# Weight loads moved to ScalarE's DMA ring, two blocks loaded ahead of the weights, a new order

## The chip, the cores and the metric

The kernel runs on one core of a Trainium2 chip. The metric is the device time of a run in microseconds (us), the median of several runs. A profiled run also has a span, from its first to its last instruction, which is about 1.9 us shorter than the time.

## The reference

```python
# attention: a recurrent state per head, (4, 8, 768, 48) inputs
state = alpha[t] * state + outer(k[t], v[t]);  y[t] = q[t] @ state
# then, with x = y as (3072, 384):
h = x @ w_in                  # w_in (384, 2048)
g = s * relu(h)**2 + b
out = g @ w_out               # w_out (2048, 384)
```

## The kernel before

The sequence is cut into 24 blocks of 128 steps, and two blocks make a group. A block needs its four inputs a (alpha), q, k and v, each 192 KB. On ScalarE it goes through `ln` and `exp`, on VectorE through the products with q and k, on TensorE (PE) through several small matmuls, and ScalarE evicts (copies out of PSUM) its y to `xd`. A group of two such blocks then goes through `mm1` (h_ps from xd and w_in), `relu`, square and `mm2` (o_ps from w_out). The weights arrive as four w_in quarters i0 to i3 and four w_out quarters o0 to o3, 768 KB each, in four staging buffers `wst`, and ScalarE casts each to bf16. An o quarter can be loaded when the cast of the i quarter in its buffer is done.

All loads are issued by SyncE, so they stand in one ring, the queue of transfers that an engine's DMA issues go into:

```python
    def load(n, src, dst):                       # block n
        nc.sync.dma_start(out=dst[n % NIN], in_=src[...])          # cut
    for src, dst in ((alpha, a_in), (q, q_in), (k, k_in), (v, v_in)):
        load(0, src, dst)
    nc.scalar.dma_start(out=b_col, in_=moe_b.to_broadcast((128, 1)))
    nc.scalar.dma_start(out=s_col, in_=moe_s.to_broadcast((128, 1)))
    def load_w_in(i, st):
        nc.sync.dma_start(out=wst[st]..., in_=moe_w_in[...])        # cut
    def load_w_out(i, st):
        nc.sync.dma_start(out=wst[st]..., in_=moe_w_out[...])       # cut
LOADS = ["b0", "i0", "i1", "b1", "i2", "b2", "b3", "i3", "o0", "o1", "o2", "o3", "b4", ...]
```

A small list scheduler at build time (`op(engine, duration, priority, function, ...)`) decides the order of each engine's instructions. Every engine then works through its own list strictly in order. Where the scheduler sees PE idle early on, it lays "fills", matmuls of zeros into o_ps that are meant to keep PE's clock up.

(A transfer has landed when its last byte has arrived and its semaphore says so.)

## Time and profile before

| | before |
|---|---|
| time | 197.4 us (196.1 to 197.5, 3 runs) |
| span of the profiled run | 195.6 us |
| PE busy | 176.8 us, of which 58 fills are 10.7 us |
| first `ln`, first mm1, first mm2 | 4.19, 22.04, 34.3 us |

The page of the kernel before, cut to PE's total, PE's granted clock and the DMA engines' busy share (tenths, in 40 slices of the span), and the group of the fills (count, then busy us and mean ns):

```profile
PE 176.8 (90%) x2126; PEld 127.6 (65%) x2126; DVE 147.8 (76%) x353; ACT 108.7 (56%) x225; POOL 35.1 (18%) x60
...
PEclk9999999999999999999999999999999999999999
DMA  5999899987999998997699988999799799410012
...
L674 PE MATMUL o_ps<-zeros,ident_bf 128*128 128x256 bf16 x58 | 10.7, 338 | 0.0
```

PE looks busy nearly everywhere, but in the first slices that is fills. The windows view of the same run, by stage (busy us of each engine, then granted clock, DMA share and GB/s):

```profile
core 0: us, PE busy (x) PEld busy (x) DVE busy (x) ACT busy (x) POOL busy (x), PEclk, DMA share, GB/s
0.00:22.00 22.00, 14.06 (x148) 9.69 (x149) 9.90 (x20) 9.75 (x15) 7.87 (x23) 1.00 0.85 209
22.00:32.00 10.00, 8.18 (x118) 6.40 (x117) 9.14 (x23) 7.50 (x15) 2.06 (x3) 1.00 1.04 270
32.00:45.00 13.00, 10.97 (x106) 7.66 (x104) 11.26 (x26) 11.47 (x18) 2.22 (x2) 1.00 0.95 260
45.00:187.00 142.00, 138.43 (x1730) 101.02 (x1729) 115.28 (x282) 79.97 (x178) 22.99 (x33) 1.00 0.85 161
```

Taking the union of PE's matmul times without the fills (overlapping times counted once), PE loses 16.1 us before 22 us, 4.5 us from there to 45, and 3.6 us in the 142 us after. So the body is bound by PE, and the front by loads. The timeline of ScalarE (start, duration, and in brackets the idle time before it and what ended it):

```profile
0.77 0.57 ACTq L202 DMA_DIRECT2D b_col<-in_moe_b_dram  x1
1.37 0.61 ACTq L203 DMA_DIRECT2D s_col<-in_moe_s_dram  x1
4.19 0.52 ACT L298 ACTIVATE la<-a_in 128x384 bf16<-128x384 f32 x1 [2.17 <-DMA a_in<-in_alpha_dram]
...
14.14 0.51 ACT L298 ACTIVATE la<-a_in 128x384 bf16<-128x384 f32 x1
...
21.49 0.49 ACT L466 ACTIVATE xd<-py_ps 128x384 bf16<-128x384 f32 x1
```

The second block's y is evicted at 21.49 us, and mm1 follows (timeline of PE):

```profile
22.04 2.16 PE L488 MATMUL h_ps<-xd,w_in_bf 128*128 128x256 bf16 x16
```

### The profile page before, as it was taken

Reading aid. Unit: us, or ns where it says so; the run is one execution under the profiler, and the core shown is the slowest. Engines: PE = TensorE matmul, PEld = TensorE weight load, DVE = VectorE, ACT = ScalarE, POOL = GpSimd, SP = SyncE. Lnnn points to the kernel's source line nnn. Section 1 sums busy time; section 2 is a strip of 40 time slices with the busy share of each in tenths; the row PEclk is TensorE's granted clock in tenths of the full one; section 3 lists DMA queues with packets and bytes.
Section 4 is the critical chain, followed back from the end, with each engine's and each line's share of the span. In section 5 each row is a group of like instructions: output and inputs, shape, how many; then the busy total and the mean of one; then the engine's idle time right before and its main releaser. Section 6 shows DMA issues by size and latency. Waiting matters only on the chain.

```text
span 195.6 us, 5398 instructions
## 1 busy us (share of the span) xinstructions
PE 176.8 (90%) x2126; PEld 127.6 (65%) x2126; DVE 147.8 (76%) x353; ACT 108.7 (56%) x225; POOL 35.1 (18%) x60
## 2 busy tenths in 40 slices
PE   0698888699998899999999799998999999999992
PEld 0466666466666767777777577676676677776861
DVE  4434699699888999798987978737898889675541
ACT  3171877895135756567467477247367267365520
POOL 8401321005103033020121220301030232000000
PEclk9999999999999999999999999999999999999999
DMA  5999899987999998997699988999799799410012
GB/s 112 269 246 256 168 241 371 335 161 168 200 205 221 200 186 156 209 186 146 135 207 164 165 178 163 200 202 167 155 221 144 169 222 157 97 40 28 16 42 80
DMA packets 123161, 34.16 MB, mean 175 GB/s; under 512 B 116480, under 2 KB 121600, under 8 KB 123136
## 3 DMA queue, kind: packets, MB, share of 16 engines
q1 hardware_dynamic: 107008, 29.89, 68.4%
q10 hardware_dynamic: 16128, 3.94, 14.4%
q8 instruction: 16, 0.26, 0.5%
q14 instruction: 9, 0.07, 0.1%
HBM read 25.17 MB, written 4.72 MB: 153 GB/s over the span
## 4 chain that ended last, share of the span: by engine, by line
PE 66%; DMA 12%; DVE 8%; SPq 6%; ACT 5%; issue 2%; ACTq 0%; DVEq 0%
PE o_ps L512 28%; PE h_ps L488 25%; SPq L194 5%; DMA wst<-in_moe_w_out_dram 5%; PE py_ps L442 5%; DMA qkT<-qk 4%; DMA wst<-in_moe_w_in_dram 3%; PE a_ps L404 3%; DVE gt L505 3%; PE ct_ps L304 2%; ACT r L497 2%; ACT w_out_bf L263 1%; PE py_ps L362 1%; DVE t L387 1%; DVE qkT L371 1%
## 5 line engine op out<-in xcount | busy, mean ns | idle before, releaser
L497 ACT ACTIVATE r<-h_ps 128x512 bf16<-128x512 f32 x96 | 55.8, 599 | 35.0 <-PE h_ps L488 17.9
L512 PE MATMUL o_ps<-w_out_bf,gt 128*128 128x384 bf16 x384 | 71.9, 326 | 1.9 <-ACT w_out_bf L263 1.8
L488 PE MATMUL h_ps<-xd,w_in_bf 128*128 128x256 bf16 x576 | 72.5, 272 | 1.2 <-ACT r L497 0.9
L505 DVE TENSOR_TENSOR gt<-r 128x256 bf16<-128x256 bf16 x192 | 54.7, 333 | 16.1 <-ACT r L497 15.7
L488 PEld LDWEIGHTS <-w_in_bf 128*128 128x128 bf16 x576 | 54.5, 98 | 11.6 <-issue 1.9
L512 PEld LDWEIGHTS <-gt 128*128 128x128 bf16 x384 | 35.8, 98 | 21.7 <-issue 1.9
L413 DVE TENSOR_TENSOR am<-a_ps,mask 128x1024 bf16<-128x1024 f32 x24 | 29.3, 1220 | 1.5 <-PE a_ps L404 1.1
L398 POOL TENSOR_TENSOR s_st<-t,blast 128x384 bf16<-128x384 bf16 x16 | 14.6, 914 | 68.3 <-DVE t L387 51.1
L325 POOL CAST vp<-v_in 128x384 bf16<-128x384 f32 x24 | 15.2, 632 | 62.4 <-DMA v_in<-in_v_dram 57.0
L466 ACT ACTIVATE xd<-py_ps 128x384 bf16<-128x384 f32 x24 | 11.8, 491 | 22.0 <-PE py_ps L442 20.1
L336 DVE TENSOR_TENSOR qk<-k_in,binv 128x384 bf16<-128x384 f32 x24 | 14.2, 591 | 8.5 <-ACT binv L321 6.8
L523 DVE SCALAR_TENSOR_TENSOR o_sb<-o_ps,s_col,bias_w 128x384 f32<-128x384 f32 x24 | 14.8, 615 | 7.2 <-PE o_ps L512 6.5
L298 ACT ACTIVATE la<-a_in 128x384 bf16<-128x384 f32 x24 | 12.5, 522 | 5.5 <-DMA a_in<-in_alpha_dram 3.8
L321 ACT ACTIVATE binv<-ct_ps 128x384 f32<-128x384 f32 x24 | 11.8, 492 | 4.5 <-PE ct_ps L309 4.3
L331 DVE TENSOR_TENSOR qk<-q_in,b_s 128x384 bf16<-128x384 f32 x24 | 13.9, 580 | 0.4 <-ACT b_s L318 0.2
L318 ACT ACTIVATE b_s<-ct_ps 128x384 f32<-128x384 f32 x24 | 12.1, 503 | 2.0 <-issue 2.0
L387 DVE TENSOR_TENSOR t<-py_ps,s_st 64x192 bf16<-64x192 f32 x32 | 11.3, 354 | 2.5 <-PE py_ps L362 2.0
L404 PE MATMUL a_ps<-qkT 64*128 64x128 bf16 x192 | 9.7, 222 | 3.6 <-DVE qkT L371 2.4
L304 PE MATMUL ct_ps<-la,U_bf 128*128 128x384 bf16 x24 | 8.0, 335 | 4.9 <-ACT la L298 4.9
L404 PEld LDWEIGHTS <-qkT 64*128 64x128 bf16 x192 | 5.5, 95 | 10.0 <-DVE qkT L371 4.5
L442 PE MATMUL py_ps<-am,vp 128*32 128x128 bf16 x384 | 9.8, 223 | 1.5 <-DVE am L413 1.5
L674 PE MATMUL o_ps<-zeros,ident_bf 128*128 128x256 bf16 x58 | 10.7, 338 | 0.0
(42 smaller groups left out, 107.6 us busy)
## 6 DMA issues: line engine op xcount, KB each, us to landing
a_in<-in_alpha_dram SPq DMA_DIRECT2D x24, 192.0 KB, 3.7
q_in<-in_q_dram SPq DMA_DIRECT2D x24, 192.0 KB, 3.8
k_in<-in_k_dram SPq DMA_DIRECT2D x24, 192.0 KB, 4.0
v_in<-in_v_dram SPq DMA_DIRECT2D x24, 192.0 KB, 3.9
out_dram<-o_sb SPq DMA_DIRECT2D x24, 192.0 KB, 2.1
wst<-in_moe_w_in_dram SPq DMA_DIRECT2D x4, 768.0 KB, 6.5
wst<-in_moe_w_out_dram SPq DMA_DIRECT2D x4, 768.0 KB, 8.9
qkT<-qk ACTq DMA_TRANSPOSE x15, 4.5
```

The source lines that it names most:

```text
L325: nc.gpsimd.tensor_copy(out=vp_sb[n % 4].rearrange("a p (x d) -> a p x d", d=D)[:, :, 0:3:2, :], in_=v_in[n % NIN].rearrange("a (p e) d -> ...
L331: nc.vector.tensor_tensor(out=qk_sb[n % 3][:, 0, :, 0:D], in0=q_in[n % NIN], in1=b_sb[n % 2], op=ALU.mult)
L336: nc.vector.tensor_tensor(out=qk_sb[n % 3][:, 1, :, 0:D], in0=k_in[n % NIN], in1=binv_sb[n % 2], op=ALU.mult,)
L398: nc.gpsimd.tensor_tensor(out=s_sb[n % 3], in0=t1_sb[n % 2], in1=bl, op=ALU.mult)
L404: nc.tensor.matmul(out=a_ps[:, e, p, :], lhsT=qkT[64 * e : 64 * e + 64, 1, p, :], rhs=qkT[64 * e : 64 * e + 64, 0, p, :], start=True, stop ...
L413: nc.vector.tensor_tensor(out=am_sb[n % 2].rearrange("a e p t -> a (e p) t"), in0=a_ps.rearrange("a e p t -> a (e p) t"), in1=mask.unsquee ...
L442: nc.tensor.matmul(out=y_ps[32 * (x % 4) : 32 * (x % 4) + 32, x // 4, :], lhsT=(st[:, p, c0 : c0 + 32] if e is None else vp[:, p, c0 + 48 ...
L488: nc.tensor.matmul(out=hp[:, i * n : (i + 1) * n], lhsT=w_in_bf[:, kk, 128 * j : 128 * (j + 1)], rhs=xd_sb[g % 3][:, kk, 0:n], start=(kk = ...
L497: nc.scalar.activation(out=r_sb[w % 2], in_=h_ps[w % 2], func=AF.Relu)
L505: nc.vector.tensor_tensor(out=gt_sb[j][:, c0 : c0 + n], in0=r, in1=r, op=ALU.mult)
L512: nc.tensor.matmul(out=op[:, 0:d_model], lhsT=gt_sb[j][:, c0 : c0 + C], rhs=w_out_bf[:, j, :], start=(j == 0), stop=(j == NJ - 1),)
L523: nc.vector.scalar_tensor_tensor(out=ots, in0=o_ps[(x // 4) % 2][:, 0:d_model], scalar=s_col, in1=bias_w, op0=ALU.mult, op1=ALU.add,)
```

## The change

The intent: give the weights a ring of their own, so that they and the blocks no longer queue behind each other on SyncE's ring; load two blocks ahead of the first quarter, so that the attention part starts early; move the two scalars out of the way; and a re-tuned order.

```diff
-UNIT = 1.396
-LEAD = {1: 72.9, 2: 87.9, 4: 83.9}
-NPE = 9
-NAY = 5
+UNIT = 5.886
+LEAD = {1: 52.5, 2: 71.9, 4: 230.0}
+NPE = 7
+NAY = 10
-TB = 1.1
-TW = 2.3
+TB = 1.02
+TW = 2.15
 # ... (cut: every priority in P has another value)
-LOADS = ["b0", "i0", "i1", "b1", "i2", "b2", "b3", "i3", "o0", "o1", "o2", "o3", "b4", "b5", "b6"]
+LOADS = ["b0", "b1", "i0", "i1", "b2", "i2", "b3", "i3", "o0", "o1", "o2", "o3", "z0", "b4", "b5", "b6"]
-    nc.scalar.dma_start(out=b_col, in_=moe_b.to_broadcast((128, 1)))
-    nc.scalar.dma_start(out=s_col, in_=moe_s.to_broadcast((128, 1)))
     def load_w_in(i, st):
-        nc.sync.dma_start(
+        nc.scalar.dma_start(
     def load_w_out(i, st):
-        nc.sync.dma_start(
+        nc.scalar.dma_start(
+    def load_bs():
+        nc.sync.dma_start(out=b_col, in_=moe_b.to_broadcast((128, 1)))
+        nc.sync.dma_start(out=s_col, in_=moe_s.to_broadcast((128, 1)))
-            op("SP", TW, t, load_w_in, i, st, w=[("wst", st)], lat=2.0)
+            op("ACT", 0.5, t, load_w_in, i, st, w=[("wst", st)], lat=0.0)
+            op("SP", TW, t, lambda: None, r=[("wst", st)], w=[("wst", st)], lat=2.0)
 # ... (cut: the same for w_out, and the op for the scalars)
```

Two details of the scheduler's side: it models an issue on ScalarE as 0.5 us, and it models the transfer as if all loads still went one after another in the order of LOADS. `NPE` is the number of blocks whose transposes PE does; the others use DMA transposes.

More of the change, by code (lines that the diff above doesn't have):

```diff
@@ L18 @@
 GROUPS = [2, 2, 2, 2, 2, 2, 2, 2, 2, 2, 2, 2]
-UNIT = 1.396
-LEAD = {1: 72.9, 2: 87.9, 4: 83.9}
-NPE = 9
-NAY = 5
+UNIT = 5.886
+LEAD = {1: 52.5, 2: 71.9, 4: 230.0}
+NPE = 7
+NAY = 10
 RING = 12
 NST = 4
-TB = 1.1
-TW = 2.3
+TB = 1.02
+TW = 2.15
 FILL_GAP = 0.45
-P_BM, P_CS, P_BMM = -5, -48.2, -221.5
+P_BM, P_CS, P_BMM = -5, 595.6, 725.9
 P = dict(
-    ln=9.85, cum=-2.97, eb=3.53, ei=-4.54, vc=-2.78, qb=15.79, kb=-10.16, T=5.42,
-    Tc=-1.09, KV=4.4, t1=4.97, sn=-0.59, Ay=-5.51, A=-4.02, mk=-10.39, y=12.28,
-    ye=-10.99, m1=3.02, re=-4.95, sq=-1.4, m2=14.39, oe=-25.12,
+    ln=-5.79, cum=20.09, eb=19.07, ei=-26.07, vc=21.99, qb=33.73, kb=-1.8, T=-23.27,
+    Tc=-9.48, KV=0.27, t1=26.65, sn=-32.67, Ay=-1.75, A=48.23, mk=25.72, y=30.39,
+    ye=19.25, m1=-18.3, re=-0.12, sq=-2.14, m2=61.6, oe=-12.26,
 )
-LOADS = ["b0", "i0", "i1", "b1", "i2", "b2", "b3", "i3", "o0", "o1", "o2", "o3", "b4", "b5", "b6"]
+LOADS = ["b0", "b1", "i0", "i1", "b2", "i2", "b3", "i3", "o0", "o1", "o2", "o3", "z0", "b4", "b5", "b6"]
 class Schedule:
@@ L560 @@
                        w=[(name, 0)], lat=2.0)
-                op("DVE", 0.3, P_BM, bias_mul, w=["bones"], lock=True)
+            continue
+        if item[0] == "z":
+            op("SP", 0.6, t, load_bs, w=["b", "s"], lat=2.3)
+            op("DVE", 0.3, P_BM, bias_mul, r=["b"], w=["bones"], lock=True)
             continue
@@ L565 @@
         if item[0] == "i":
-            op("SP", TW, t, load_w_in, i, st, w=[("wst", st)], lat=2.0)
+            op("ACT", 0.5, t, load_w_in, i, st, w=[("wst", st)], lat=0.0)
+            op("SP", TW, t, lambda: None, r=[("wst", st)], w=[("wst", st)], lat=2.0)
             op("ACT", 1.4, -500, cast_w_in, i, st, r=[("wst", st)], w=[("wib", i)])
         else:
-            op("SP", TW, t, load_w_out, i, st, w=[("wst", st)], lat=2.0)
+            op("ACT", 0.5, t, load_w_out, i, st, w=[("wst", st)], lat=0.0)
+            op("SP", TW, t, lambda: None, r=[("wst", st)], w=[("wst", st)], lat=2.0)
             op("ACT", 1.4, -400, cast_w_out, i, st, r=[("wst", st)], w=[("wob", i)])
```

## The prediction

> **What bounds the kernel now.** The profile's span is 195.6 us (time 197.4). The page gives PE 90% busy, but 10.7 us of that are the 58 fill matmuls (o_ps from zeros). Without them, the union of PE's matmuls is about 168 us, so about 28 us are lost. Summing by windows: 16.1 us are lost before 22 us, 2.3 in 22 to 32, 1.8 in 32 to 38, only some 3.5 from 45 to 187, and 3.9 in the tail. So the body is PE-bound; the front is bound by loads. The timeline shows the first mm1 (h_ps) at 22.04 and the first mm2 (o_ps from w_out) at 34.3, right after the fourth block's y. From then on PE waits little (1.8 us for w_out casts).
>
> In the front the 16 DMA engines are saturated (DMA share 0.96 in 2 to 26 us). By the windows, blocks alone move at 206 GB/s (768 KB in about 3.6 us, an estimate from it), weights alone at 337 to 377 GB/s (768 KB in about 2.2 us). The queue stalls in single issues: k_in 3.6 and 3.9 us, q_in 2.6, the four w_out issues 7.1.
>
> **What the change does.** Eight 768 KB weight loads move to ScalarE's ring. By the order of ScalarE's program the four w_in quarters are issued ahead of everything, at about 0.8 us, and each w_out load follows the cast that frees its buffer. SyncE issues blocks 0 to 3 back to back, then the two scalars. The Trainium skill, "DMA: Bandwidth & Descriptors", section "Issuing engines are not separate DMA queues", says both rings run on the same 16 engines and interleave, and two issuers save issue time only. No run here shows it yet for weights beside blocks. I take it: four blocks and four quarters are about 23 us of transfers whatever the ring. Block 0 should land later (v_in cast at 9 to 13 us, not 6.6), because w_in now competes with it; block 1 at about 16 to 18, much as before; the w_out quarters earlier, since nothing stalls behind a full ring (last cast at 33 to 38 us, not 40.5). ScalarE pays about 8 x 0.6 us of issue, off the path.
>
> Two PE transposes of blocks become DMA transposes (17 instead of 15): 2 x 0.6 us less PE and 2 x 0.69 us less VectorE, where VectorE is 19.0 of 20 us busy (60 to 80 us). The order has 45 fills instead of 58, and the same sequence up to the first mm2. Rest: reshuffled priorities, perhaps 1 us either way.
>
> **Sum (estimates).** Transposes -1.2; w_out waits -1; fewer stalls ahead of the fourth block -1 (-5 if blocks win the shared engines, +2 if weights do); better order after 45 us -0.5. From 197.4 I expect 193.7 us.
>
> **Would show it right:** first mm1 at 18 to 22 us, first mm2 at 30 to 34.5; block 0's v_in cast later than 6.6; no ScalarE or PE wait on w_out beyond 1 us; PE busy 176 or less with about 8 us of fills; loss between 45 us and the tail at 3.5 us or less.
>
> **What would make it wrong:** w_in descriptors (2 KB) crowding out the blocks' 192 B ones, so block 0 lands after 12 us, first mm1 comes after 24 us, and the time stays or rises; ScalarE, in order, blocked by a weight issue or by a cast ahead of a relu; a later stretch where the new order makes PE wait on the DMA transposes. Or blocks keep most of the rate: first mm1 at 16 us and a time near 190.
>
> Chances: faster by over 2% 0.48, within 2% 0.43, slower 0.09. Range 188.5 to 198.5 us.

## More of the kernel before

The build gives the DMAs of both rings eight completion semaphores in turn, so a DMA waits, before it is issued, until the DMA that had its semaphore before (usually eight places earlier) has landed. That wait stands in the stream of the issuing engine.

The clock line needs care. The trace has no clock record before 15.48 us (22.60 us in the changed kernel), and the page draws that as full speed. The fills, all of one size, tell otherwise: two timeline groups of them, on either side of the first record, are

```profile
12.27 3.58 PE L674 MATMUL o_ps<-zeros,ident_bf 128*128 128x256 bf16 x17
15.95 1.47 PE L674 MATMUL o_ps<-zeros,ident_bf 128*128 128x256 bf16 x12
```

Their starts are 213 ns apart in the first group and 109 ns apart in the second, so until about then PE ran at half its later rate.

## The result

| | before | after |
|---|---|---|
| time, median | 196.76 us (4 runs) | 205.73 us (205.21 to 205.98, 4 runs) |
| ratio to before | | 1.0457 (1.0394 to 1.052) |
| span of the profiled run | 195.6 us | 203.8 us |
| first `ln`, first mm1, first mm2 | 4.19, 22.04, 34.3 us | 10.64, 30.49, 45.3 us |
| last w_out cast starts | 40.5 us | 50.0 us |
| fills | 58, 10.7 us | 45, 8.6 us |

A ratio here, and in every experiment below, is the mean time of one kernel's fast runs over that of the kernel before in the same rounds, with a 95% interval, so it is not quite the ratio of the medians. The medians are over all runs; in e3, e10, e13, e15 and e16 they include one slow run. Differences in us below are of medians, some from different rounds. By the ratios the gains over the changed kernel are 9.5 us (e1), 6.0 (e2), 4.9 (e3), 4.3 (e15), 1.8 (e17) and 1.1 (e9), each give or take 1.5 to 3 us (estimates from the ratios and their intervals).

The page after:

```profile
PE 177.7 (87%) x2097; PEld 127.0 (62%) x2097; DVE 146.8 (72%) x351; ACT 108.5 (53%) x225; POOL 32.2 (16%) x60
...
PEclk9999985999999999999999999999999999999999
DMA  5999979992019999699699988998998597301112
```

The windows after:

```profile
core 0: us, PE busy (x) PEld busy (x) DVE busy (x) ACT busy (x) POOL busy (x), PEclk, DMA share, GB/s
0.00:22.00 22.00, 8.99 (x82) 5.91 (x83) 8.60 (x19) 6.22 (x12) 6.95 (x23) 1.00 1.00 255
22.00:32.00 10.00, 4.63 (x59) 3.31 (x58) 1.82 (x3) 3.10 (x7) 0.97 (x2) 0.87 0.88 195
32.00:45.00 13.00, 11.72 (x140) 8.96 (x139) 9.90 (x23) 9.62 (x15) 2.69 (x4) 0.84 1.02 245
45.00:187.00 142.00, 139.25 (x1733) 99.98 (x1729) 120.12 (x288) 85.22 (x187) 21.61 (x32) 1.00 0.82 163
```

The whole loss lies before 45 us. More bytes are moved before 22 us than before (255 against 209 GB/s), and yet PE works less. After 45 us the changed kernel is no worse: without the fills PE loses 2.8 us there, against 3.6. From 24 to 30 us all compute engines are nearly idle at once (PE is busy for 1.12 us, VectorE, ScalarE and GpSimd for 0.05 us or less). The timeline of ScalarE shows two holes:

```profile
0.77 9.82 ACTq L240 DMA_DIRECT2D wst<-in_moe_w_in_dram  x4
10.64 0.52 ACT L300 ACTIVATE la<-a_in 128x384 bf16<-128x384 f32 x1 [8.62 <-DMA k_in<-in_k_dram]
...
18.73 1.48 ACT L248 ACTIVATE w_in_bf<-wst 128x1536 bf16<-128x1536 f32 x1
21.42 0.38 ACTq L255 DMA_DIRECT2D wst<-in_moe_w_out_dram  x1
21.85 1.49 ACT L248 ACTIVATE w_in_bf<-wst 128x1536 bf16<-128x1536 f32 x1 [1.65 <-DMA k_in<-in_k_dram]
23.24 0.51 ACT L300 ACTIVATE la<-a_in 128x384 bf16<-128x384 f32 x1
29.47 0.38 ACTq L255 DMA_DIRECT2D wst<-in_moe_w_out_dram  x1
29.95 0.49 ACT L468 ACTIVATE xd<-py_ps 128x384 bf16<-128x384 f32 x1 [6.20 <-DMA v_in<-in_v_dram]
```

The brackets hold the clue. The first `ln` reads a alone, yet the landing of k ended its wait. The eviction to `xd` reads y from PSUM alone, which PE had finished at 23.5 us, yet the landing of a v ended its wait. Neither instruction needs those loads; the DMA issues standing ahead of them do. The trace has the landings: i2, i3, o0, o1 and o2 went out at 6.45, 10.21, 21.42, 29.47 and 37.20 us, and the loads named below had landed at 6.43, 10.19, 21.34, 29.40 and 37.12. The built program agrees, listing for each weight load the previous user of its semaphore:

```
place among the DMAs   load   semaphore   previous user, which must have landed
 8                     i2     0           a of block 0
11                     i3     3           k of block 0
22                     o0     6           k of block 2
27                     o1     3           v of block 3
34                     o2     2           v of block 4
```

PE pays in two ways, as its timeline shows:

```profile
24.85 0.27 PE L681 MATMUL o_ps<-zeros,ident_bf 128*128 128x256 bf16 x1
30.49 4.00 PE L490 MATMUL h_ps<-xd,w_in_bf 128*128 128x256 bf16 x18 [5.37 <-ACT xd L468]
```

It waits 5.37 us, and then its clock has dropped: the clock record is 0.50 from 29.42 to 36.25 us, and the 18 matmuls take 4.00 us. In the trace as a whole, of 8.2 us more span, 5.0 us are PE's idling and fills and 3.1 us are longer matmul time (171.0 us of matmuls without fills, against 167.9). PE also first reached full rate later, at 22.60 us instead of 15.48.

Two theories came out of this. A: ScalarE's in-order stream stands behind weight issues. B: on the shared DMA engines the w_in loads, now in flight from the start, crowd the blocks. A third, C: the new order and priorities lose the time.

### The profile page after: what moved, and what is told of

Same layout as the page of the kernel before. It is cut to its first block, busy times and chain, and to the rows that moved or that the text cites. A ratio compares the mean times of both kernels' runs of the same rounds, so it can differ in the third digit from the quotient of the medians.

```text
span 203.8 us, 5352 instructions
## 1 busy us (share of the span) xinstructions
PE 177.7 (87%) x2097; PEld 127.0 (62%) x2097; DVE 146.8 (72%) x351; ACT 108.5 (53%) x225; POOL 32.2 (16%) x60
## 4 chain that ended last, share of the span: by engine, by line
PE 58%; DVE 13%; SPq 11%; DMA 8%; ACT 5%; issue 2%; ACTq 0%; DVEq 0%
PE h_ps L490 24%; PE o_ps L514 23%; SPq L194 11%; DVE gt L507 5%; PE py_ps L444 4%; DMA v_in<-in_v_dram 4%; PE a_ps L406 3%; DVE am L415 2%; DMA k_in<-in_k_dram 2%; DMA q_in<-in_q_dram 2%; DVE t L389 2%; DVE o_sb L525 2%; ACT r L499 2%; DMA a_in<-in_alpha_dram 1%; ACT w_out_bf L261 1%
## 5 line engine op out<-in xcount | busy, mean ns | idle before, releaser
L490 PE MATMUL h_ps<-xd,w_in_bf 128*128 128x256 bf16 x576 | 76.0, 278 | 5.4 <-ACT xd L468 5.4
L507 DVE TENSOR_TENSOR gt<-r 128x256 bf16<-128x256 bf16 x192 | 55.3, 335 | 16.9 <-ACT r L499 16.1
L338 DVE TENSOR_TENSOR qk<-k_in,binv 128x384 bf16<-128x384 f32 x24 | 13.5, 564 | 18.9 <-ACT binv L323 17.1
L400 POOL TENSOR_TENSOR s_st<-t,blast 128x384 bf16<-128x384 bf16 x16 | 13.7, 854 | 76.5 <-DVE t L389 44.1
L327 POOL CAST vp<-v_in 128x384 bf16<-128x384 f32 x24 | 13.3, 556 | 64.1 <-DMA v_in<-in_v_dram 46.5
L311 PEld LDWEIGHTS <-la 128*128 128x128 bf16 x96 | 6.0, 98 | 12.5 <-issue 10.5
```

What stands on the lines that cost most here:

```text
L400: nc.gpsimd.tensor_tensor(out=s_sb[n % 3], in0=t1_sb[n % 2], in1=bl, op=ALU.mult)
L490: nc.tensor.matmul(out=hp[:, i * n : (i + 1) * n], lhsT=w_in_bf[:, kk, 128 * j : 128 * (j + 1)], rhs=xd_sb[g % 3][:, kk, 0:n], start=(kk = ...
L507: nc.vector.tensor_tensor(out=gt_sb[j][:, c0 : c0 + n], in0=r, in1=r, op=ALU.mult)
```

## The experiments

Fifteen kernels ran, all correct. "All-SyncE" below means that every weight load is issued by SyncE at its place in LOADS. In the first three the scheduler's plan is unchanged, so every engine keeps the order that the changed kernel gives it, apart from the issues that move.

### e1_both_sp: the rings undone, all else kept

```diff
-op("ACT", 0.5, t, load_w_in, ...); op("SP", TW, t, lambda: None, ...)
+op("ACT", 0.5, t, lambda: None, ...); op("SP", TW, t, load_w_in, ...)   # and nc.sync; same for w_out
```

> The changed kernel with all eight weight loads issued by SyncE again, at the places of its own load order (b0, b1, i0, i1, b2, ...); every engine's order else as after. Theory A (ScalarE's in-order stream stands behind weight issues that wait for other loads to land): first ln at about 4.2 us instead of 10.6, no ScalarE gap before the second xd (6.2 us after), first h_ps matmul at 17 to 21 us instead of 30.5, time 190 to 196 us. Rival B (w_in merely crowds the blocks on the shared engines): cured too, same numbers. Rival C (the new order and priorities are the loss): time stays at 203 or more.

Measured: 196.63 us, ratio 0.9975 (0.9898 to 1.0051). Just above the expected range. First `ln` at 3.61 us, first mm1 at 18.79. The holes are gone and 9.1 us come back, so C falls: the rings are the whole loss, within the intervals. But the time only equals before's. The first mm1 is 3.3 us earlier, and PE gives it back: it loses 5.5 us from 22 to 32 us (before: 2.3), 3.5 us of the run's waits being for w_in casts that now come late behind blocks. Its matmuls without fills also take 170.3 us, 2.4 more than before; its clock record is 0.50 from 37.13 to 40.54 us. The start of its list of PE's waits (us in total, times, longest):

```profile
PE ct_ps L306 <- ACT la L300: 4.2, 1, 4.2
PE h_ps L490 <- ACT w_in_bf L248: 3.5, 2, 1.9
```

### e2_wout_sp and e3_win_sp: one half of the weights on each ring

```diff
 # e2: load_w_out by SyncE as in e1, load_w_in stays on ScalarE
 # e3: load_w_in by SyncE as in e1, load_w_out stays on ScalarE
```

> Only the four w_out loads back on SyncE; w_in stays on ScalarE. Theory A: first ln still at about 10.6 us, but the 6.2 us ScalarE gap ahead of the second xd is gone, first h_ps matmul at about 24 us, no dip of the granted clock, time about 198 us (196 to 200). Rival B: w_out on the other ring is not the cost, time 203 or more. Rival C: 203 or more.

Measured: 200.0 us, ratio 1.0151 (1.0074 to 1.0228). First `ln` still at 10.82 us, but the eviction at 23.67, first mm1 at 25.03, and the clock, at full rate from 22.58 us on, does not drop in the front. So, with w_out moved back first, w_out on ScalarE's ring costs 5.7 us, and w_in 3.4 (200.0 against 196.6).

> Only the four w_in loads back on SyncE; w_out stays on ScalarE. Theory A: first ln at about 4.2 us, first h_ps matmul at 17 to 22 us unless a w_out issue waits for a late block load on the way, time 191 to 197 us. Rival B: the same, since w_in does not compete with block 0. Rival C: 203 or more.

Measured: 201.46 us, ratio 1.0207 (1.0076 to 1.0338), higher than expected. First `ln` 3.70, first mm1 18.52 us, no long hole at an issue before that. Yet the last w_in cast starts at 34.38 us (e1: 30.86) and the k product of block 2 at 21.39 (19.43). The first two w_out issues go out at 15.25 and 17.41 us, ahead of v of block 2, i2, block 3 and i3, and k of block 2, already issued, lands at 21.30 us (e1: 19.03). That looks like crowding again: w_out, needed last, overtakes what is needed first; no run tests it apart from ScalarE's waits. Moving w_in alone to ScalarE costs 3.4 us, w_out alone 4.8 (4.6 by the ratios); both together cost 9.1.

### e4_before_act: the ring alone, on the kernel before

```diff
-op("SP", TW, t, load_w_in, i, st, w=[("wst", st)], lat=2.0)
+op("ACT", 0.5, t, load_w_in, ...); op("SP", TW, t, lambda: None, ...)   # and nc.scalar; same for w_out
```

> The kernel before, with its own order and priorities, and only the eight weight loads moved to ScalarE's ring. Again all four w_in issues stand ahead of the first ln. Theories A and B: first ln at 10 us or later, time 201 to 208 us. Rival C: about 197 us, as before, since the order is the old one.

Measured: 208.16 us, ratio 1.0541 (1.0451 to 1.0631), just above the range of A and B and far from C's. The four w_in issues take ScalarE from 2.02 to 13.13 us, the first `ln` starts at 13.23 and the first mm1 at 34.33. The new ring harms the old order just as well.

### e6_i23_late, e7_pairs, e8_i0123_late: blocking or crowding at the start

All three start from e2.

```diff
 # e6: i2 and i3 issued on ScalarE after block 0's exps
     def st_exp_b(n):
         nc.scalar.activation(out=b_sb[n % 2], in_=cum_ps, func=AF.Exp)
+        if n == 0:
+            load_w_in(2, 2); load_w_in(3, 3)
 # e8: all four there
 # e7: w_in as two double loads (3 x 1024 columns each), so neither issue waits for a semaphore
+        nc.scalar.dma_start(out=wpair[st // 2]..., in_=moe_w_in[:, 512 * i : 512 * (i + 2)]...)
```

> As the run with w_out on SyncE (200.0 us), but the third and fourth w_in quarter are issued on ScalarE behind block 0's ln and exps, so only two quarters share the engines with block 0 and ScalarE has nothing to wait for ahead of the first ln but its data. Theory A (ScalarE's stream blocked): first ln at about 6.4 us (the landing of a_in), first k product at about 8.5, first h_ps matmul at 20 to 23, time 196 to 199 us. Rival B (crowding decides): first k product at 10 us or later, first h_ps matmul and time as in the w_out run, 25 us and 200 us.

Measured: 199.08 us, ratio 1.012 (1.007 to 1.0169). The `ln` moved to 6.37 us, the k product to 10.21, but the first mm1 stayed at 25.10.

> As the run with w_out on SyncE (200.0 us), but the four quarters come as two double loads, so all of w_in is in flight at once and neither issue waits for anything: crowding at its largest, blocking gone. Theory A: first ln at about 6.4 us, first k product by 9 us, first h_ps matmul by 22 us, time 196 to 198 us. Rival B: block 0's q, k, v land after 11 us although the first ln is early; first h_ps matmul at 24 us or later, time 199 to 203 us.

Measured: 199.91 us, ratio 1.0139 (1.0082 to 1.0197). Theory A fails this one. Its timeline of ScalarE shows a stream that is free after 1.89 us and an `ln` that waits for its own data:

```profile
0.77 1.12 ACTq L250 DMA_DIRECT2D wst<-in_moe_w_in_dram  x2
10.50 0.52 ACT L308 ACTIVATE la<-a_in 128x384 bf16<-128x384 f32 x1 [8.48 <-DMA a_in<-in_alpha_dram]
```

> As the run with w_out on SyncE (200.0 us), but all four w_in issues stand behind block 0's exps on ScalarE: block 0 shares the engines with nothing. Theory A and B both: first ln at about 4.2 us, first k product at about 6.5. A: the issues now wait for loads of block 0 and 1 in front of block 1's ln, which starts at 11 us or later. First h_ps matmul at 20 to 24 us, time 196 to 200 us; if blocking hardly matters and crowding is all, 195 to 197.

Measured: 199.47 us, ratio 1.0148 (1.0105 to 1.019). Block 0 is as early as before (k product at 5.62 us), and block 1 pays instead: its `ln` at 16.09, its k product at 18.94. Here ScalarE's stream is blocked again, as A said: block 1's a had landed at 7.15 us, but three issues stand ahead of the `ln`:

```profile
6.46 9.53 ACTq L240 DMA_DIRECT2D wst<-in_moe_w_in_dram  x3
16.09 0.52 ACT L300 ACTIVATE la<-a_in 128x384 bf16<-128x384 f32 x1 [10.42 <-DMA a_in<-in_alpha_dram]
```

Crowding is there too: block 1's k landed at 14.36 us, against 9.70 in e1.

What follows: with w_in issued at the start, B holds. In e2, e6 and e7 block 1's k lands at 17.8 to 18.2 us whether ScalarE is blocked (e2) or not (e7), against 9.70 in e1, and its k product starts at 17.9 to 19.9 us, against 11.01. In e1 and then e6:

```profile
11.01 0.55 DVE L338 TENSOR_TENSOR qk<-k_in,binv 128x384 bf16<-128x384 f32 x1
17.86 0.56 DVE L341 TENSOR_TENSOR qk<-k_in,binv 128x384 bf16<-128x384 f32 x1 [0.98 <-DMA k_in<-in_k_dram]
```

The times of e2, e6, e7 and e8 lie between 199.1 and 200.0 us, so issuing later (e8) only exchanged one cause for the other. The trace's DMA packets show how the blocks are crowded. From 3 to 5 us the changed kernel moves 355 packets of 192 B from SyncE's ring and 312 of 2048 B from ScalarE's: nearly one for one, so 0.07 MB of blocks to 0.64 MB of weights. The kernel before moves 2019 block packets in those 2 us. In e7, with 4096 B packets, it is 212 to 160 and a lands still later (`ln` at 10.50 us, against 6.37 in e6); e7 also has all four quarters in flight and e6 two, so packet size alone is not tested.

### e9_o1_after_xd1: the second hole, one instruction moved

```diff
     def st_yevac(n):
         nc.scalar.activation(out=xd_sb..., in_=y_ps, func=AF.Copy)
+        if n == 1:
+            load_w_out(1, 1)
```

> The changed kernel with one ScalarE instruction moved: the issue of the second w_out quarter stands behind the eviction of block 1's y instead of ahead of it. Same loads, same rings. Theory A: that eviction at about 23.7 us instead of 29.95, first h_ps matmul at about 24.3 instead of 30.5; the relu behind the issue then waits to about 29.5 us, so only part comes back: time 201 to 204.5 us. Rival B (late data, not the stream's order): no change, 205 to 206.5 us.

Measured: 204.63 us, ratio 1.0403 (1.0362 to 1.0444). The eviction is at 23.95 and the first mm1 at 25.45, as A says, but the issue still goes out at 29.31 and now the `exp` of block 2 and the `relu` stand behind it. About 1 us came back, not clear of noise and just short of what A allowed (201 to 204.5 us); what A has here is the trace. It does not exclude B for w_out, hence the next two.

### e15_o1_sp and e17_o01_one: the second hole, one load and one semaphore

```diff
 # e15: o1 alone issued by SyncE; the other seven stay on ScalarE
+        (nc.sync if i in (1,) else nc.scalar).dma_start(
 # e17: o0 and o1 as one double load on ScalarE, issued after the second w_in cast
+        nc.scalar.dma_start(out=wpair[0]..., in_=moe_w_out[0:1024, :]...)
```

> The changed kernel with one load alone, the second w_out quarter, issued by SyncE instead of ScalarE; the other seven stay on ScalarE. Theory A (the 6.2 us gap is ScalarE's stream behind that one issue, which reuses the semaphore of block 3's v): gap gone, first h_ps matmul at 24 to 26 us instead of 30.5, time 199 to 202 us, most of the 5.7 us that moving all four gave. Theory B (w_out crowds the blocks on the shared engines): one quarter of that, 203.5 to 205.5 us.

Measured: 200.86 us, ratio 1.0236 (1.0119 to 1.0353). Moving one load gives back 4.9 of the 5.7 us that moving all four gave (4.3 of 6.0 by the ratios), and the first mm1 is at 25.73 us. It also shifts the semaphores of the loads after it in the program: o0 waits for another one and goes out at 20.25 instead of 21.42 us. ScalarE in this run:

```profile
22.15 0.51 ACT L300 ACTIVATE la<-a_in 128x384 bf16<-128x384 f32 x1
24.26 0.49 ACT L468 ACTIVATE xd<-py_ps 128x384 bf16<-128x384 f32 x1 [1.60 <-PE py_ps L444]
```

The eviction now waits for PE, which makes its input.

> The changed kernel with the first two w_out quarters as one double load, still on ScalarE, issued after the second w_in cast. In the built program it reuses the semaphore of block 3's a (issued 19.3 us in the changed kernel's trace), not of its v. Same bytes, same ring. Theory A: ScalarE goes on at about 23 us, first h_ps matmul at 24 to 26 us, time 199 to 203 us. Theory B: w_out still shares the engines with block 3, so 204.5 to 207 us.

Measured: 202.79 us, ratio 1.0365 (1.0268 to 1.0463). By time alone this is not clear of the changed kernel (1.0394 to 1.052); the trace decides. The same bytes on the same ring, and the hole is gone with the semaphore: first mm1 at 26.06 us. The wait moved in part to the next issue, o2, which reuses the semaphore of block 4's k:

```profile
30.38 0.51 ACT L309 ACTIVATE la<-a_in 128x384 bf16<-128x384 f32 x1
33.61 0.45 ACTq L258 DMA_DIRECT2D wst<-in_moe_w_out_dram  x1
34.16 0.60 ACT L508 ACTIVATE r<-h_ps 128x512 bf16<-128x512 f32 x1 [3.27 <-DMA k_in<-in_k_dram]
```

After that second hole the clock record is 0.50 again, from 35.32 to 38.73 us. So for w_out in the changed kernel A holds: one issue on ScalarE, waiting for a semaphore last used by a block load, costs some 4 to 5 us.

### e12_before_npe7: my term for the transposes

```diff
-NPE = 9
+NPE = 7      # on the kernel before
```

> The kernel before with NPE 7 instead of 9 alone: two more blocks transposed by DMA. My prediction's term: 1.2 us less PE work, so 195 to 196.5 us if PE bounds the body; 196.5 to 199 us if the two DMA transposes make PE wait for them.

Measured: 202.25 us, ratio 1.0294 (1.0224 to 1.0364), outside both. The front is the same (first mm1 21.96 us); from 60 to 187 us PE loses 7.1 us where before lost 3.2. Only 1.1 us of all its waits is for a DMA transpose; 3.8 us are mm1 waiting for `relu`. The scheduler re-plans everything when a block's transpose moves, so this run is not the cost of two transposes alone, and I cannot say which reordering it is. One candidate I overlooked: a DMA transpose is itself an issue on ScalarE, and each took 1.25 to 2.65 us of its stream in this trace. At least three of PE's waits after 60 us (0.42, 0.63 and 1.12 us) end at the ScalarE instruction right behind one. That this is the loss is not shown. It shows that 2 x 0.6 us of PE work could not be booked as a gain by itself.

### e10, e11, e13, e16: can the front's gain be kept?

```diff
 # e10 (on e1): i2 ahead of b2, i3 ahead of b3 in LOADS
 # e11 (on e1): TB = 1.1, TW = 2.3, the load times of before
 # e13 (on e1): both
 # e16 (on before): the changed kernel's LOADS alone
```

> The all-SyncE version of the changed kernel (196.6 us) with the third and fourth w_in quarter one block earlier in the load order (i2 ahead of b2, i3 ahead of b3). If PE's 3.5 us of waiting for w_in casts there come from the load order: those waits under 1 us, w_in casts 2 and 3 by 21 and 29 us, time 193 to 196 us. If the block loads are the limit instead, y of block 3 comes later by as much and the time stays at 196 to 198.

Measured: 198.01 us, ratio 1.007 (0.9993 to 1.0147). The w_in casts came as expected (17.97 and 24.24 us) and the first mm2 at 33.02 instead of 36.07 us, but PE loses more later.

> The all-SyncE version (196.6 us) with the scheduler's load times of the kernel before (1.1 and 2.3 us instead of 1.02 and 2.15), so it plans on longer waits and lays more fills between 23 and 36 us. If the granted clock's dip there (about 0.7 to 0.8 in two slices) comes from PE's idling: no dip, h_ps matmuls back to before's pace, time 193.5 to 196 us. If not, 196 to 198.

Measured: 198.79 us, ratio 1.0135 (1.0069 to 1.0202). The clock's dip went, as expected, and the time did not: the expectation missed.

> Both at once: w_in quarters one block earlier and the load times of the kernel before, all on SyncE. Candidate to beat both kernels: 191.5 to 195 us if both gains are real; 195 to 198 if neither is.

Measured: 205.82 us, ratio 1.047 (1.0394 to 1.0546), a plain miss. Its first mm1 is the earliest of all, at 16.95 us, and PE loses 8.2 us from 60 to 187 us (before: 3.2). The scheduler's reordering of the body outweighs the front.

> The kernel before with the changed kernel's load order alone (b0, b1, i0, i1, b2, ...), all on SyncE, the scalars early, the old priorities. First h_ps matmul 2 to 4 us earlier than 22.0. If the load order alone is worth that: 194 to 196 us. If the gain is lost again to later w_in quarters, as in the all-SyncE version: 196 to 198.5 us.

Measured: 195.50 us, ratio 0.9967 (0.9863 to 1.0072). First mm1 at 17.57 us, 4.5 us earlier than before, and the time is the same as before's within the interval. No version here is shown to beat the kernel before.

## Why the prediction was wrong

I predicted 193.7 us (188.5 to 198.5); it was 205.7.

1. The step that failed: "ScalarE pays about 8 x 0.6 us of issue, off the path." I took an issue's length from issues that wait for nothing. I had named ScalarE "blocked by a weight issue" among what would make me wrong, but gave it no term in the sum. On ScalarE the first four held the stream from 0.77 to 10.59 us, and o1 held it from the end of the `ln` at 23.75 until 29.47. That o1 hole alone costs 4.9 us (e15; 4.3 by the ratios), about as much as the whole gain I forecast (3.7). The program's waits were there to be read before the run; I read only the order.
2. "No run here shows it yet for weights beside blocks. I take it: four blocks and four quarters are about 23 us of transfers whatever the ring." The Trainium skill, "DMA: Bandwidth & Descriptors", section "Issuing engines are not separate DMA queues", says that both rings run on the same 16 engines and interleave. The traces agree: the busy share was 1.00 in the first 22 us. The error was to reason from the total and not from who goes first. The same page, section "Queues, rings and completion order", says that each engine goes round robin between rings by packet. With 2048 B beside 192 B that gave the weights about nine times the bytes (0.64 to 0.07 MB in 3 to 5 us). (What the trace counts as a packet is one run of 192 or 2048 B; the page's packet can hold several, so the trace shows only that their numbers are nearly equal.) This costs 3.4 us (e2 against e1; e6 and e7 say that it is not the blocked `ln`). I had named it as the thing that would make the prediction wrong, with block 0 after 12 us and mm1 after 24: the v cast came at 13.25 us and mm1 at 30.49. The term "fewer stalls ahead of the fourth block -1" had the wrong sign: that block's y was evicted at 45.46 us instead of 34.24 (both holes lie before it).
3. "w_out waits -1" and "the w_out quarters earlier": the last w_out cast came at 50.0 us, not at 33 to 38. In e1, without the ring, it came at 41.4, so the load order did not bring it forward either.
4. "Transposes -1.2": not shown. e12 alone got slower, by a re-planned body, and the term left out ScalarE's time for the issues.
5. "Better order after 45 us -0.5": about right, 2.8 us lost there instead of 3.6.
6. Not counted at all: PE's wait let its clock drop to 0.50 for 6.83 us. The Trainium skill, "TensorE: Matmul & The Clock Gate", Part 1, gives half rate after an idle window of about 3.4 us; the 5.37 us wait and the 0.50 agree.

Shown by experiment: the rings are the whole loss (e1, e4); o1's issue is most of w_out's part (e15, e17); crowding, not the blocked first `ln`, is w_in's part (e6, e7; in e8 a blocked `ln` of block 1 takes its place). Argued only: how the 3.1 us of longer matmul time divide between the slow clock and other causes. Matmuls without fills ran for 11.4 us at half rate, against 3.1 before; at full rate they would take some 4 us less (an estimate from these two), which would cover it. But e11 has 171.0 us of matmuls too, with 6.6 us at half rate and no drop, so it stays open. Open: which of the body's reorderings make e12 and e13 slow.

## What to carry to other kernels

A DMA issued from an engine that computes stands in that engine's stream with all its waits, so read the waits of the built program, its reused semaphores too, before calling an issue cheap. Here a second ring moved more bytes early (255 against 209 GB/s before 22 us), but they were the wrong ones: it let the weights overtake, at nine times the blocks' bytes. So keep loads that are needed in a known order on one ring, or test it. In a trace, an instruction whose wait was ended by a load that it does not read can be the sign of another instruction ahead of it.

## What the Trainium skill lacked or had wrong

- "DMA: Bandwidth & Descriptors", "Issuing engines are not separate DMA queues": says what concurrent issuing saves, not what it can cost on an engine that computes. Elsewhere the page does say that the wait for a semaphore is the issuing sequencer's, without a cost for it. Here four issues held ScalarE for 9.82 us and one for 5.7 us, where an issue without a wait took 0.5 to 0.6 us.
- The same page, "Queues, rings and completion order", has the round robin by packet but not its result for rings of unequal packets: 355 packets of 192 B to 312 of 2048 B in 2 us, and a block's first input used at 6.4 us (2048 B, two quarters in flight, e6) or 10.5 us (4096 B, four in flight, e7) instead of 4.2.
- The same page asks for one semaphore per transfer in flight for correctness. No page has the time that reuse costs: moving one load whose semaphore was last used by an unrelated one gave back 4 to 5 us (e15).
- "TensorE: Matmul & The Clock Gate", Part 1, gives about 3.4 us of sustained work until full rate, counted in windows that run freely. The trace agrees: the half-rate record of 6.83 us is two such windows, and PE was busy for 2.34 us of the first and all of the second. What the page lacks is how idle a window must be for the clock to drop: in e1 it dropped at 37.13 us after 3.41 us of which PE was busy for 1.68, with no idle stretch above 1.7 us.
